# Attention and gated layer in one kernel: ACT's casts behind the copies of sums, output DMAs behind their copies, a tile's third bank last

## Chip, cores and metric

The kernel runs on one NeuronCore of one Trainium2 chip. The metric is the device time of one execution in microseconds (us), the median of several runs. Each execution that was profiled also leaves a trace of every instruction on the engines: TensorE (PE; its weight loads are listed as PEld), VectorE (DVE), ScalarE (ACT), GpSimd (POOL) and SyncE (SP), which issues DMAs. "ACTq" and "SPq" are an engine's sequencer, which issues DMAs and waits.

## The reference

```python
# q, k, v: (8, 8, 576, 64) float32;  w_in: (512, 2048);  w_out: (2048, 512)
scores = np.matmul(q, k.transpose(0, 1, 3, 2)) / 8
scores = np.where(block(row) >= block(column), scores, -1e9)      # blocks of 64
attn = softmax(scores)                                            # over the last axis
x = np.matmul(attn, v)  ->  tokens (4608, 512): head outputs side by side
h = x @ w_in
g = h * (1 / (1 + np.exp(-1.702 * h)))
out = g @ w_out                                                   # (4608, 512) float32
```

## The kernel before, in words

**Two streams of work.** The attention handles 32 pairs of heads (`NPAIR`), four pairs (`HP`) for each of the eight batch entries. The second layer handles 12 tiles of 384 tokens (`TILES`), each with 16 groups (`fc`) of 128 of the 2048 hidden columns. TensorE's order of both is fixed by the program: every matmul is pinned behind the one written before it (`mm`). The main loop writes the items of a pair (from strings such as `ORDER`), and after each item lets the generator `moe()` run until its quota of work is used up, so both streams alternate on TensorE.

**Attention, a step.** Pairs 0 to 7 are "early", pairs 8 to 31 "late". In a late step `n`, TensorE computes scores of chunks 3, 0, 2, 1 of pair `n`; then `N` and `T` scale and turn the weights of what was scored; then `V` is `av(n - 1)`: 60 matmuls of turned weights with values into two sum banks `o0` and `o`, and behind them the scores of chunk 4 of the next pair `m`, part of them into free columns of the same two banks. Then ACT copies the sums from `o0` and `o` to `xr` (L550, L551), SP loads the next values (L309, L312), and `settle(m, [[4]], ...)` handles the scores of chunk 4: for each head DVE's score reduction with mask and maximum (L432), ACT's exp with row sum (L439). In `settle` before the change, `prep(n + 1)` is called after these, ahead of scaling (L448 to L460) and turning (L467, L472 on DVE, then 16 DMAs on SP, L479, into `turned`).

**Preparing queries and keys.** For pairs 9 to 31, `prep` is `prep_late`: for queries (x = 0) and keys (x = 1) DVE transposes the raw data (L322, into `qt` and over `raw`), ACT casts to the rounded half `high` (L323), and POOL subtracts to get `low` in two pieces (L88, `low<-qt,high` and `low<-raw,high`). Score matmuls use both halves in three products. Then `prep` has SP load the raw data of a later pair (L301, eight DMAs).

**The second layer, a tile.** `split(t)` makes the halves `xh` (ACT, L602) and `xl` (DVE, L88) of the tile's tokens from `xr`. For each group `fc`, twelve matmuls go into `hp` (four column blocks with `xh` twice and `xl` once; in group 0 those with `xl` come last); ACT makes a tanh of it (L666), DVE the gated `g` (L667), ACT the rounded half `gh` (L675), POOL the rest `gl` (L88). One group later, `second` adds nine matmuls into the sums `acc0`, `acc1`, `acc2`, three 128-token banks, three products each: `gh` with `woh`, `gh` with `wol`, `gl` with `woh`. In all groups but the last, the six with `gh` come first and the three with `gl` behind them. After the last group each bank is copied to an output tile `osb` by ACT (L632), and ACT issues the DMA to HBM (L634). There are two `osb` buffers, and a third for the last tile only. The next tile uses the same three banks.

**What sets the order on the other engines.** The order of instructions of ACT, DVE, POOL and SP is made when the kernel is built, by a planner: it goes through the program with estimated durations and, whenever an engine is free, takes the ready instruction of highest priority. Earlier written means higher priority, and `high_priority(offset=300)` (around `split`, the tanh, `g`, `gh` and `gl`) treats an instruction as if it were written 300 places earlier. An instruction whose data are ready early in the planner's view can so be placed ahead of others that were written before it. `tc.keep_in_program_order(x)` pins `x` behind the last instruction written before it on the same engine, in issue order only. On the chip each engine then executes that order, and waits on semaphores for data, free buffers and DMA landings.

Of the kernel before, what the change touches and what calls it, by code (L numbers as in the profile page):

```python
# [41 lines left out]
def attention_moe_kernel(  # L42
# [9 lines left out]
    nc = tc.nc  # L52
    B, H, S, D = q.shape
    DM, DF = w_in.shape
    P = 128
# [8 lines left out]
    NPAIR = B * H // 2  # L64
# [8 lines left out]
    def f(ap):  # L73
        return ap.bitcast(F32)
# [59 lines left out]
    def room(tag, shape, dt, name):  # L134
        return d2.tile(shape, dt, tag=tag, name=name, bufs=1)
# [62 lines left out]
    for g in range(NG):  # L198
# [3 lines left out]
        for fc in range(FG):  # L202
            r = (g * FG + fc) * P
# [31 lines left out]
    bits, whole = {}, {}  # L235
# [78 lines left out]
    high, low = {}, {}  # L314

    def prep_late(n):

        high[n] = [room(t, [P, S], F32R, "high") for t in ("wm", "high")]
        low[n] = room("qk", [P, 2, S], F32R, "low")
        for x in range(2):  # L320
            whole = raw[n][:, 0].rearrange("p c d -> p (c d)") if x else room("e1", [P, S], F32, "qt")
            nc.vector.transpose(out=whole, in_=raw[n][:, x].rearrange("p c d -> p (c d)"))  # L322
            nc.scalar.copy(out=high[n][x], in_=whole)  # L323
            for c in (slice(0, S // 2), slice(S // 2, S)):
                subtract(nc.gpsimd, low[n][:, x, c], whole[:, c], f(high[n][x])[:, c])

# [15 lines left out]
    def prep(n):  # L342

        if not parts_of(n):
            qk[n] = room("e0" if n % 2 else "qk", [P, 2, S], F32, "qk")
            for x in range(2):
                nc.vector.transpose(out=qk[n][:, x], in_=raw[n][:, x].rearrange("p c d -> p (c d)"))
        else:
            prep_late(n)
        raw.pop(n)  # L350
        m = follower(n)
        if m is not None:
            load(m)
# [30 lines left out]
    def settle(n, banks, todo):  # L384
        for chunks, part in zip(banks, todo):
            e = {}
            for i, hd, lo, hi, s in part:
                if i not in e:
                    e[i] = es[i] if early(n) else weights_of(n, i)
                weigh(n, i, hd, lo, hi, s, e[i])  # L390
            if early(n):
                for i in chunks[::-1]:
                    if n == 2 * HP - 1 and i == NCH - 1:
                        with tc.high_priority(offset=300):
                            normalise(n, i, e[i])
                    else:
                        normalise(n, i, e[i])
            else:
                weighed.extend((n, i, e[i]) for i in chunks[::-1])
            if 4 in chunks and not early(n):  # L400
                if n + 1 < NPAIR:
                    prep(n + 1)
                normalise_all()
                turn_all()

# [105 lines left out]
    def av(n):  # L511

        b, h = divmod(n, HP)
        before_av(n)
        if turns["late"]:
            o0, o = bank(), bank()
            cut = BLK + 2 * P
        else:
            o, o0 = bank(), bank()
            cut = BLK  # L520

        def place(q0):
            return (o0, q0) if q0 < cut else (o, q0 - cut)

        todo = []
        for i in range(1, NCH):
            bk, c = place((i - 1) * P + BLK)
            todo += [(bk, c, P, j, pw[:, :, SLOT[i] + j]) for j in range(i)]
            todo.append((bk, c + BLK, BLK, i, pw[:, 2:4, 9 + i]))
        todo.append((*place(0), BLK, 0, pw[:, 0:2, 10]))  # L530

        ends = [[x for x, y in enumerate(todo) if y[0] is bk] for bk in (o0, o)]
        for x, (bk, c, nn, j, w) in enumerate(todo):
            for hd in range(2):
                mm(
                    out=bk[hd * D : hd * D + D, c : c + nn].rearrange("d (a c) -> d a c", c=32),
                    lhsT=values(n)[:, hd, j], rhs=w[:, :, hd],
                    start=any(x == y[0] for y in ends), stop=any(x == y[-1] for y in ends),
                )
        m = n + 1  # L540
        rest = []
        if turns["late"] and m < NPAIR:
            own = [lent_bank(), bank()]
            a, z = qrange(4)
            beside = [o0[:, cut : cut + S - K4], o[:, S - cut : S - cut + S - K4]]
            for ss, lo, hi in (([x[:, 0:K4] for x in own], 0, K4), (beside, K4, S)):
                score_into(m, a, ss, lo, hi)
                rest += [(4, hd, lo, hi, ss[hd][0 : z - a]) for hd in range(2)]
        c0 = (b % 2) * S
        nc.scalar.copy(out=xr[:, h, c0 : c0 + cut], in_=o0[:, 0:cut])  # L550
        nc.scalar.copy(out=xr[:, h, c0 + cut : c0 + S], in_=o[:, 0 : S - cut])  # L551
        nxt = follower(n)
        if nxt is not None:
            load_v(nxt)
        if rest:
            settle(m, [[4]], [sorted(rest, key=lambda x: x[2])])

    def follower(n):
# [54 lines left out]
    def moe():  # L613
        prev = None

        def second(state):
            g_hi, g_lo, fc, acc, t = state
            todo = [(c, ga, wb) for c in range(TILES[t][1] // P) for ga, wb in ((g_hi, "woh"), (g_hi, "wol"), (g_lo, "woh"))]
            if fc < NFC - 1:

                todo.sort(key=lambda x: x[1] is g_lo)
            begun = set()
            for x, (c, ga, wb) in enumerate(todo):
                last = ga is g_lo
                mm(
                    out=acc[c], lhsT=ga[:, c * P : (c + 1) * P], rhs=weights(wb, fc // FG)[:, fc % FG],
                    start=fc == 0 and c not in begun, stop=fc == NFC - 1 and last,
                )
                begun.add(c)
                if fc == NFC - 1 and last:  # L630
                    osb = out_room([P, DM], F32, "osb", t == NT - 1)
                    nc.scalar.copy(out=osb, in_=acc[c])  # L632
                    r = TILES[t][0] + c * P
                    nc.scalar.dma_start(out=out[r : r + P, :], in_=osb)  # L634
                if x % 3 == 2:
                    yield 650

        for t in range(NT):
            tt = TILES[t][1]
            if t == 0:  # L640
                yield ("tile", 0)
                split(0)
            xh, xl = xs["xh"], xs["xl"]
            acc = [ps.tile([P, DM], F32, tag=f"acc{c}", name=f"acc{c}") for c in range(tt // P)]
            for fc in range(NFC):
                if t == 0:
                    convert(fc // FG * GROUP + NDC + fc % FG + 1)
                hp = next_hp()
                fs = slice(fc % FG * P, (fc % FG + 1) * P)
                terms = [(wa, xb, dc) for dc in range(NDC) for wa, xb in (("wih", xh), ("wil", xh), ("wih", xl))]  # L650
                if fc == 0:

                    terms.sort(key=lambda x: x[1] is xl)
                for cnt, (wa, xb, dc) in enumerate(terms):
                    mm(
                        out=hp[:, 0:tt], lhsT=weights(wa, fc // FG)[:, dc, fs], rhs=xb[:, dc, 0:tt],
                        start=cnt == 0, stop=cnt == 3 * NDC - 1,
                    )
                    if cnt % 3 == 2:
                        yield unit1(tt)  # L660
                g = d2.tile([P, TT], F32, tag="g", name="g", bufs=1)[:, 0:tt]
                gh = d2.tile([P, TT], F32R, tag="gh", name="gh")[:, 0:tt]
                gl = d2.tile([P, TT], F32R, tag="gl", name="gl")[:, 0:tt]

                with tc.high_priority(offset=300):
                    nc.scalar.activation(out=g, in_=hp[:, 0:tt], func=AF.Tanh, scale=1.702)  # L666
                    nc.vector.scalar_tensor_tensor(  # L667
                        out=g, in0=g, scalar=1.0, in1=hp[:, 0:tt], op0=ALU.add, op1=ALU.mult
                    )

                if fc == NFC - 1 and t + 1 < NT:
                    yield ("tile", t + 1)
                    split(t + 1)
                with tc.high_priority(offset=300):
                    nc.scalar.copy(out=gh, in_=g)  # L675
                    subtract(nc.gpsimd, gl, g, f(gh))
                yield ("gate", fc)
                if prev is not None:
                    yield from second(prev)
                prev = (gh, gl, fc, acc, t)  # L680
        yield from second(prev)


# [85 lines left out]
```

## Time and profile before

| | |
|---|---|
| median of 3 runs | 1099.38 us (1098.8 to 1101.41) |
| the profiled execution's own time | 1097.82 us |
| its span, first to last instruction | 1096.0 us |
| granted TensorE clock, mean | 0.991 |
| busy: PE, PEld, DVE, ACT, POOL | 1058.2, 928.2, 597.5, 522.0, 477.9 us |
| HBM read, written | 45.09 MB, 9.44 MB |

Busy time is a share of the whole span, over stages with different limits. A row of an instruction group or of the timeline names line, engine, operation, `out<-in` tiles and shapes; the bracket at its end is the idle time of the engine just before it and what ended that. A helper's line stands for all its callers: L114 is every matmul, L88 every subtraction. In a row of stretches stand the length, then busy time and number of instructions of PE, PEld, DVE, ACT and POOL, then the granted clock, the DMA share and GB/s. A row of waits names who waited for whom, then the total in us, how often, and the longest.

### The profile page before, as it was taken

The page shows a single profiled execution, that of the slowest core. Times are in us where ns is not written, and L with a number is a line of the kernel's source. Part 1 is how long each engine was busy: PE and PEld are TensorE (multiplying, and loading weights), DVE is VectorE, ACT ScalarE, POOL GpSimd, SP SyncE. Part 2 cuts the span into 40 slices and gives each one's busy share as a digit, 9 for nine tenths or more (in the row PEclk, how much of TensorE's full clock was granted, in tenths as well). Part 3 has the DMA queues.
Part 4 walks back from the last instruction along what each step waited for, and adds up shares of the span by engine and source line. Part 5 has one row for each costly group of instructions (what it writes and reads, how often), then busy time and mean ns, then how long its engine had stood idle before and what let it go on. Part 6 is the DMA issues. An engine that isn't in the chain of part 4 may idle for free. (4 is left out here: it accounts for less than half of the span.)

```text
span 1096.0 us, 20723 instructions
## 1 busy us (share of the span) xinstructions
PE 1058.2 (97%) x7236; PEld 928.2 (85%) x7236; DVE 597.5 (55%) x1856; ACT 522.0 (48%) x1367; POOL 477.9 (44%) x601
## 2 busy tenths in 40 slices
PE   5869999999999999999999999999999999999998
PEld 3647777888889888899898888998898888999997
DVE  6786786755655656655655665655556655211111
ACT  5866776533544544534444543443544443322322
POOL 4665665534444444344344443443444343222222
PEclk9979999999999999999999999999999999999999
DMA  8735523433333443332434343333444322200000
GB/s 174 210 91 156 151 60 81 98 69 80 92 79 77 111 92 79 83 82 67 105 81 87 85 107 62 78 89 76 106 97 88 66 79 48 55 30 1 30 1 30
DMA packets 219369, 91.30 MB, mean 83 GB/s; under 512 B 197760, under 2 KB 197760, under 8 KB 219264
## 3 DMA queue, kind: packets, MB, share of 16 engines
q1 hardware_dynamic: 209344, 79.94, 32.3%
q10 hardware_dynamic: 9920, 10.03, 2.6%
q8 instruction: 57, 0.93, 0.4%
q14 instruction: 48, 0.39, 0.1%
HBM read 45.09 MB, written 9.44 MB: 50 GB/s over the span
## 5 line engine op out<-in xcount | busy, mean ns | idle before, releaser
L88 POOL TENSOR_TENSOR gl<-g,gh 128x384 fp32r<-128x384 f32 x192 | 195.0, 1016 | 454.5 <-ACT gh L675 442.4
L667 DVE SCALAR_TENSOR_TENSOR g<-g,hp 128x384 f32<-128x384 f32 x192 | 104.9, 546 | 359.7 <-ACT g L666 359.6
L114 PE MATMUL hp<-xh,wih 128*128 128x384 f32 x768 | 260.9, 340 | 4.5 <-DVE g L667 2.2
L114 PE MATMUL hp<-xh,wil 128*128 128x384 f32 x768 | 258.3, 336 | 0.0
L114 PE MATMUL hp<-xl,wih 128*128 128x384 f32 x768 | 254.3, 338 | 0.1
L114 PE MATMUL acc<-woh,gh 128*128 128x512 f32 x576 | 232.8, 404 | 2.7 <-ACT osb L632 2.2
L114 PE MATMUL acc<-wol,gh 128*128 128x512 f32 x576 | 227.5, 395 | 0.0
L666 ACT ACTIVATE g<-hp 128x384 f32<-128x384 f32 x192 | 93.7, 488 | 247.5 <-PE hp L114 215.4
L675 ACT CAST gh<-g 128x384 fp32r<-128x384 f32 x192 | 98.5, 513 | 167.9 <-DVE g L667 167.3
L114 PE MATMUL acc<-woh,gl 128*128 128x512 f32 x576 | 168.7, 394 | 0.3 <-POOL gl L88 0.3
L114 PEld LDWEIGHTS hp<-xh,wih 128*128 128x128 f32 x768 | 144.5, 188 | 17.9 <-issue 3.3
L114 PEld LDWEIGHTS hp<-xh,wil 128*128 128x128 f32 x768 | 144.3, 188 | 7.7
L114 PEld LDWEIGHTS hp<-xl,wih 128*128 128x128 f32 x768 | 143.7, 188 | 1.1 <-DVE xl L88 1.1
L439 ACT ACTIVATE e<-e,mx 64x64 f32<-64x64 f32 (+4 forms) x240 | 132.4, 554 | 18.4 <-DVE mx L432 18.4
L114 PEld LDWEIGHTS acc<-woh,gh 128*128 128x128 f32 x576 | 108.0, 188 | 27.1 <-ACT osb L632 4.0
L114 PEld LDWEIGHTS acc<-woh,gl 128*128 128x128 f32 x576 | 107.6, 188 | 25.9 <-POOL gl L88 2.1
L458 POOL TENSOR_TENSOR e<-e,sm 64x64 f32<-64x64 f32 (+1 forms) x192 | 112.9, 613 | 34.0 <-DVE sm L453 23.1
L114 PEld LDWEIGHTS acc<-wol,gh 128*128 128x128 f32 x576 | 108.4, 188 | 16.9 <-issue 0.4
L448 DVE TENSOR_SCALAR sm<-sm 128x2 f32<-128x2 f32 (+1 forms) x160 | 64.6, 404 | 63.6 <-ACT e L439 57.3
L432 DVE CUSTOM_DVE_ANT_0 e<-bank,mask 64x64 f32<-64x64 f32 (+4 forms) x240 | 93.2, 438 | 4.8 <-PE bank L114 4.6
L114 PEld LDWEIGHTS bank<-turned,vp 128*64 128x64 f32 x1800 | 85.4, 137 | 9.6 <-issue 6.6
L114 PE MATMUL bank<-turned,vp 128*64 128x128 f32 (+1 forms) x1800 | 89.6, 257 | 1.6 <-ACT turned L493 1.6
(62 smaller groups left out, 1205.1 us busy)
## 6 DMA issues: line engine op xcount, KB each, us to landing
turned<-turned SPq DMA_DIRECT2D x192, 80.0 KB, 2.1
turned<-turned SPq DMA_DIRECT2D x96, 112.0 KB, 2.2
raw<-in_q_dram SPq DMA_DIRECT2D x128, 72.0 KB, 2.3
out_dram<-osb ACTq DMA_DIRECT2D x36, 256.0 KB, 2.1
raw<-in_k_dram SPq DMA_DIRECT2D x120, 72.0 KB, 2.4
turned<-turned SPq DMA_DIRECT2D x96, 88.0 KB, 2.1
words<-in_moe_w_in_dram SPq DMA_DIRECT2D x16, 512.0 KB, 5.9
vp<-in_v_dram SPq DMA_DIRECT2D x60, 128.0 KB, 2.5
```

The source lines that it names most:

```text
L88: eng.tensor_tensor(out=out, in0=in0, in1=in1, op=ALU.subtract)
L114: return tc.keep_in_program_order(nc.tensor.matmul(**kw))
L432: nc.vector.tensor_tensor_reduce(out=e[0:m, hd, lo:hi], in0=s, in1=mk, op0=ALU.add, op1=ALU.min, scale=-0.125, scalar=3e38 if lo == 0 else ...
L439: nc.scalar.activation(out=e[0:m, hd], in_=e[0:m, hd], func=AF.Exp, scale=-1.0, bias=mx[0:m, i, hd : hd + 1], accum_out=sm[0:m, i, hd : hd ...
L448: x = nc.vector.tensor_scalar(out=c, in0=c, scalar1=1e-9, scalar2=2.0, op0=ALU.add, op1=ALU.mult)
L458: nc.gpsimd.tensor_tensor(out=x, in0=x, in1=sc.to_broadcast([m, width(i)]), op=ALU.mult)
L666: nc.scalar.activation(out=g, in_=hp[:, 0:tt], func=AF.Tanh, scale=1.702)
L667: nc.vector.scalar_tensor_tensor(out=g, in0=g, scalar=1.0, in1=hp[:, 0:tt], op0=ALU.add, op1=ALU.mult)
L675: nc.scalar.copy(out=gh, in_=g)
```

## The change

The casts L323 are pinned behind what is written before them on ACT. `prep(m + 1)` moves from `settle` to `av`, to the place just behind the copies of the sums and the loading of values, ahead of `settle`; so the last ACT instruction written before the first cast is the copy L551. In group 0 of a tile, `second` takes the three products of bank 2 behind all six of banks 0 and 1 (their `gh` products first, then their two `gl` products, then bank 2's). The output DMAs L634 are pinned behind what is written before them on ACT, their own copy.

```diff
@@ prep_late
-            nc.scalar.copy(out=high[n][x], in_=whole)
+            tc.keep_in_program_order(nc.scalar.copy(out=high[n][x], in_=whole))
@@ settle
             if 4 in chunks and not early(n):
-                if n + 1 < NPAIR:
-                    prep(n + 1)
                 normalise_all()
                 turn_all()
@@ av
         if rest:
+            if m + 1 < NPAIR:
+                prep(m + 1)
             settle(m, [[4]], [sorted(rest, key=lambda x: x[2])])
@@ second
             if fc < NFC - 1:
-                todo.sort(key=lambda x: x[1] is g_lo)
+                todo.sort(key=lambda x: (fc == 0 and x[0] == 2, x[1] is g_lo))
@@ second, after the last group
-                    nc.scalar.dma_start(out=out[r : r + P, :], in_=osb)
+                    tc.keep_in_program_order(nc.scalar.dma_start(out=out[r : r + P, :], in_=osb))
```

## The prediction

> **What bounds the kernel now.** I read the page's first part, then busy time by stretches, then TensorE's waits.
>
> ```profile
> span 1096.0 us, 20723 instructions
> PE 1058.2 (97%) x7236; PEld 928.2 (85%) x7236; DVE 597.5 (55%) x1856; ACT 522.0 (48%) x1367; POOL 477.9 (44%) x601
> ```
> ```profile
> 0.00:190.00 190.00, 161.19 (x1173) 124.75 (x1174) 140.99 (x434) 132.71 (x369) 113.04 (x141) 0.96 0.53 133
> 190.00:1050.00 860.00, 855.02 (x5859) 766.42 (x5859) 450.92 (x1413) 377.62 (x977) 354.73 (x451) 1.00 0.33 76
> ```
>
> TensorE (PE, the first busy number of each row) is the bound; ScalarE (ACT) works under half the time. Of the 37.8 us in which PE is idle, 28.8 lie before 190 us, and 4.0 after 1050, where only the last tile runs and no wait is touched. Before 190 the change alters only the order of nine matmuls of tile 0: casts in halves begin with pair 9, output copies with the end of tile 0, and both come after 190. From 190 to 1050, where nearly all edits act, PE is idle for 860.00 - 855.02 = 5.0 us. So the gain is capped near 5 us, 0.45%. What TensorE waits for in that stretch:
>
> ```profile
> PE acc L114 <- ACT osb L632: 2.2, 3, 0.8
> PE hp L114 <- ACT xh L602: 1.6, 1, 1.6
> ```
>
> The first is the output sums' third bank, not yet copied out when the next tile wants it; the second is one wait at tile 1's start. Together 3.8 of the 5.0 us, and each has an edit aimed at it.
>
> **The third bank (edit at L621).** The three waits are at tiles 3, 6 and 9 and alike (2.2 us over three, the longest 0.8). Tile 3, on ACT, POOL and PE (start, duration):
>
> ```profile
> 374.32 0.56 ACT L632 COPY osb<-acc 128x512 f32<-128x512 f32 x1
> 375.24 0.51 ACT L675 CAST gh<-g 128x384 fp32r<-128x384 f32 x1 [0.36 <-DVE g L667]
> 375.30 0.34 ACTq L634 DMA_DIRECT2D out_dram<-osb  x1
> 375.68 0.59 ACT L632 COPY osb<-acc 128x512 f32<-128x512 f32 x1
> 376.30 0.34 ACTq L634 DMA_DIRECT2D out_dram<-osb  x1
> 377.37 0.58 ACT L632 COPY osb<-acc 128x512 f32<-128x512 f32 x1 [1.10 <-DMA out_dram<-osb]
> ```
> ```profile
> 376.31 1.01 POOL L88 TENSOR_TENSOR gl<-g,gh 128x384 fp32r<-128x384 f32 x1
> ```
> ```profile
> 376.87 0.39 PE L114 MATMUL acc<-wol,gh 128*128 128x512 f32 x1
> 378.00 0.51 PE L114 MATMUL acc<-woh,gh 128*128 128x512 f32 x1 [0.75 <-ACT osb L632]
> 378.34 0.40 PE L114 MATMUL acc<-wol,gh 128*128 128x512 f32 x1
> 378.58 0.86 PE L114 MATMUL acc<-woh,gl 128*128 128x512 f32 x3
> 379.29 0.33 PE L114 MATMUL hp<-xh,wih 128*128 128x384 f32 x1
> ```
>
> Matmuls into the sums start every 0.24 us (378.34 to 378.58); the first after a wait takes 0.34 (378.00 to 378.34). The third bank is wanted at 376.87 + 0.24 = 377.11, fifth in order; its copy ends at 377.95, and PE starts 378.00. With the edit, fifth and sixth are the matmuls with gl for banks 0 and 1, and the third bank is wanted two steps later. But gl ends at 376.31 + 1.01 = 377.32, not by 377.11: a new wait of about 0.26 takes part of the old one's place. Then 377.37, 377.71 and, at 377.95, the third bank, whose copy ends just then: start 378.00, after it 0.34, 0.24, 0.24 to the group's end at 378.82 instead of 379.29. Gain 0.47 a tile. Had the copy come earlier (next part), the end would be 378.67 and the gain 0.62. In the other tiles PE shows no wait for the copy, so nothing is gained, and gl is made long before the new fifth matmul, so nothing is lost. Sum: 3 x 0.47 = 1.4 us.
>
> **Output DMAs behind their copies (L634).** The edit pins a DMA behind the last ACT instruction written before it, which is its own copy; by data it follows it already. In the rows above the first DMA stands behind copy and gh cast: the copy ended 374.88, gh waited for VectorE until 375.24, the DMA left at 375.30. If the pin changes nothing, 0. If the DMAs move right behind their copies, that one leaves at 374.92, lands 0.38 earlier, and the third copy, which waits for that landing, starts 0.38 earlier: 0.15 more per tile. The price is that ACT, which issues in order, stands until the copy has ended and the DMA is out (0.34); behind the third copy waits the next tanh, 0.5 us later, whose gh is needed only after the next hp group, the twelve matmuls that start at 379.29 in the rows. I take 0, since the pin adds no order that the data do not, and keep 3 x 0.15 = 0.45 us of gain for the range.
>
> **Casts pinned, prep earlier (L323, L554).** What moves: per late pair two DVE transposes, two ACT casts, four POOL subtractions, eight raw loads on SP. Where it matters once, at tile 1's start (ACT, PE, DVE):
>
> ```profile
> 197.89 0.51 ACT L675 CAST gh<-g 128x384 fp32r<-128x384 f32 x1 [3.65 <-DVE g L667]
> 199.71 0.67 ACT L323 CAST high<-qt 128x576 fp32r<-128x576 f32 x1 [1.30 <-DVE qt L322]
> 200.52 0.67 ACT L323 CAST high<-raw 128x576 fp32r<-128x576 f32 x1
> 201.10 0.42 ACT L550 COPY xr<-bank 128x320 f32<-128x320 f32 x1
> 201.41 0.38 ACT L551 COPY xr<-bank 128x256 f32<-128x256 f32 x1
> 201.68 0.52 ACT L602 CAST xh<-xr 128x384 fp32r<-128x384 f32 x1
> ```
> ```profile
> 196.10 1.24 PE L114 MATMUL bank<-qk 64*128 64x384 f32 x8
> ```
> ```profile
> 200.33 0.34 PE L114 MATMUL hp<-xh,wil 128*128 128x384 f32 x1
> 202.25 0.44 PE L114 MATMUL hp<-xh,wih 128*128 128x384 f32 x1 [1.58 <-ACT xh L602]
> ```
> ```profile
> 202.23 0.94 DVE L88 TENSOR_TENSOR xl<-xr,xh 128x384 fp32r<-128x384 f32 x1
> ```
>
> The sums were ready at 197.34, yet their copies stand behind two casts that wait for transposes; the xh cast that TensorE needs stands behind the copies. With the casts after the copies, gh ends 198.40, copies 199.1, xh 199.6: ready before PE wants it at 200.50, and 202.25 - 200.50 = 1.75 us go. What is late next is xl, made on DVE: wanted at 201.4 (200.50, two matmuls and three of xl at 0.175), now begun at 202.23 behind the chunk's score reductions (L432). If it keeps its place, it ends about 202.5 (two of those reductions wait less for the copies), so 1.1 us stay and 0.65 are gained; if it goes ahead of them, all 1.75. I take 1.0, nearer the lower end: the first two reductions are ready with the scores, before the copies are.
>
> In the other 22 late steps the copies also wait for a cast. One step:
>
> ```profile
> 514.77 0.27 PE L114 MATMUL bank<-low,high 64*128 64x192 f32 x2
> ```
> ```profile
> 515.81 0.68 ACT L323 CAST high<-raw 128x576 fp32r<-128x576 f32 x1 [2.99 <-DMA vp<-in_v_dram]
> ```
> ```profile
> 517.55 0.79 ACT L439 ACTIVATE e<-e,mx 128x576 f32<-128x576 f32 x1
> ```
>
> ACT is idle 2.99 us ahead of the cast, yet PE runs on with earlier groups. The scores end at 515.04, so copies would run 515.1 to 515.8, casts to 517.0, and the exp starts 0.3 to 0.5 us earlier than 517.55. No TensorE wait hangs on it: 0. The raw key goes from first to second cast, its subtractions and the raw loads behind them on SP up to 1.5 us later, with the 16 turning DMAs queued behind; they are read a step later, so 0 again, but see the last rival.
>
> **The sum.** 1.4 + 1.0 = 2.4 us: span 1096.0 to 1093.6, profiled time 1097.82 to 1095.4. The median of the runs, 1099.38, lies 1.56 above the profiled one: 1097.0, or -0.22%. The ends: 0.65 + 1.4 = 2.05 us and 1.75 + 1.4 + 0.45 = 3.6 us.
>
> **Rivals.** A difference within 0.3% (3.3 us) is about what a measurement of this kernel cannot tell from no change.
>
> (1) Full gain. DMAs leave right behind their copies and xl runs promptly: 3.6 us, and with the small waits of the stretch (5.0 - 3.8 = 1.2, if they end on ACT's chains) up to 4.8. Time 1094.6 to 1095.8. For it: ACT has room, and these waits are most of what is left. Against it: nothing forces xl ahead of the reductions.
>
> (2) Hidden anyway. The third copy slips by the 0.3 to 0.5 us that ACT stands at DMAs, and new short waits on gl and xl stay: gain 0 to 1 us, 1098.4 to 1099.4. For it: gl is already late by 0.2 at the three tiles.
>
> (3) Slower, by one mechanism: the turning DMAs on SP (L479) held by an output's DMA.
>
> ```profile
> SPq L479 <- DMA out_dram<-osb: 31.1, 12, 7.0
> ```
> ```profile
> 364.64 18.85 SPq L479 DMA_DIRECT2D turned<-turned  x16
> ```
> ```profile
> 616.40 18.66 SPq L479 DMA_DIRECT2D turned<-turned  x16
> ```
> ```profile
> turned<-turned SPq DMA_DIRECT2D x192, 80.0 KB, 2.1
> ```
> ```profile
> 385.67 2.99 PE L114 MATMUL bank<-turned,vp 128*64 128x128 f32 x60
> ```
> ```profile
> DMA to landing us min/median/max: 2.0/2.1/4.4
> ```
>
> At tiles 3 and 6 the sixteen take over 18 us because they stand up to 7.0 us until an output DMA has landed. At tile 3 the last is issued some 0.6 us before 383.49 and lands 2.1 later, at 385.0: 0.65 us before TensorE reads it. If the pins rearrange the queues so that SP waits for the third output's DMA (after the third copy, at 377.95 or later) and not the first's (375.30), and that DMA takes the longest landing of the outputs (the last row), 4.4 us instead of 2.0, the turned weights come 2.65 + 2.4 = 5.05 us later and TensorE stands 4.4 us at each of two tiles: 8.8 - 2.4 = +6.4, 1105.8. It decides beyond 0.65 us of delay, and outweighs the gains where the delay passes 1.85 us. Against it: with the first output DMA's place unchanged, SP waits as now.
>
> ```profile
> 60.00:65.00 5.00, 2.08 (x12) 1.64 (x10) 3.51 (x7) 2.45 (x6) 3.17 (x3) 0.50 0.88 138
> ```
> ```profile
> PE bank L117 <- ACT xr L550: 2.9, 1, 2.9
> ```
>
> TensorE's clock would make such stalls dearer: in the stretch from 60 to 65 us, with a wait of 2.9 us in it, the granted clock is 0.50, and five us at half speed cost up to 2.5 more, so 5 over both tiles and 1110.8. The Trainium skill, "TensorE: Matmul & The Clock Gate", section "HAM oscillation — how this bites in real kernels", sets the limit at idle gaps of about 3.4 us: by it a stall of 4.4 slows the clock too, but one under 3.4 costs only itself. The trace is the harsher of the two, as its 2.9 us were enough after an earlier idle spell. Either way the waits of today's late part, under 2 us, stand at clock 1.00, and the forecast's sum gets nothing from the clock.
>
> **How the numbers follow.** Forecast (2.05 to 3.3 us gained) 0.51, full gain 0.27, hidden 0.11, slower 0.11. Predicted 1097.0. Faster by over 0.3%: the full gain and the forecast's edge, 0.33; slower 0.11; the rest 0.56. The range leaves out the slow case and the full gain's last part: 1094.3 to 1100.4, where the top takes in the hidden case and the scatter of the runs shown.
>
> **What would show it.** Right: the wait of acc for osb at tiles 3, 6, 9 gone, a wait for gl of 0.2 to 0.3 there; on ACT, L550 and L551 ahead of both casts in every late step; hp's wait for xh at 200 us gone or replaced by one for xl under 1.1; PE idle between 190 and 1050 near 2.6 us. Wrong: PE waits at av's first matmul, or idle time elsewhere that the planner's new order made.

## The result, and the profile after

The changed kernel takes 1105.76 us (median of 6 runs, 1104.23 to 1107.27) against 1098.7 us for the kernel before beside it (6 runs): ratio 1.0063, 95% interval 1.005 to 1.0075. The forecast was 1097.0 us in a range of 1094.3 to 1100.4, so it was wrong, in sign too. The rival on the slower side, with a chance of 0.11, had 1105.8.

The profiled execution of the kernel after took 1107.27 us, the slowest of the six; so the two profiled executions lie 9.45 us apart and the medians 7.06. Its first lines, then busy time by stretches:

```profile
span 1105.5 us, 20704 instructions
PE 1061.2 (96%) x7236; PEld 933.4 (84%) x7236; DVE 594.8 (54%) x1856; ACT 526.3 (48%) x1367; POOL 477.5 (43%) x601
```
```profile
0.00:190.00 190.00, 161.42 (x1174) 124.83 (x1174) 140.99 (x436) 133.10 (x371) 113.46 (x142) 0.96 0.53 133
190.00:1050.00 860.00, 848.38 (x5810) 762.94 (x5810) 447.12 (x1409) 379.48 (x971) 351.81 (x448) 0.99 0.33 76
```

The first stretch is as before. From 190 to 1050 us TensorE's idle time goes from 5.0 to 11.6 us, and the mean clock from 1.00 to 0.99. What TensorE waits for there, from its list of waits, and two rows of SP's list:

```profile
PE bank L114 <- DMA turned<-turned: 9.2, 4, 3.6
...
PE hp L114 <- DVE xl L88: 1.7, 1, 1.7
```
```profile
SPq L301 <- POOL low L88: 57.2, 22, 2.9
SPq L477 <- DMA out_dram<-osb: 48.0, 12, 9.9
```

The three waits for `osb` and the one for `xh` are gone. In their place stand one for `xl` and, new, four at the first matmul of `av`, for the DMAs that turn the weights: 2.30 us at tile 2, 1.12 at tile 3, 2.21 at tile 5 and 3.57 at tile 8. SP (L477 is L479 of before) now stands 48.0 us ahead of these DMAs until an output's DMA has landed; before it was 31.1.

Tile 2 shows the whole chain. The sixteen turning DMAs of that step, before and after, then the last two of them after:

```profile
271.01 10.06 SPq L479 DMA_DIRECT2D turned<-turned  x16
```
```profile
270.54 18.90 SPq L477 DMA_DIRECT2D turned<-turned  x16
```
```profile
288.30 1.14 SPq L477 DMA_DIRECT2D turned<-turned  x2
```

They start 0.5 us earlier than before, and still the last leaves 8 us later: fourteen go out one behind the other, and two stand until 288.30. ACT and PE of the kernel after at that moment:

```profile
285.64 0.59 ACT L632 COPY osb<-acc 128x512 f32<-128x512 f32 x1
286.12 0.52 ACT L675 CAST gh<-g 128x384 fp32r<-128x384 f32 x1
286.25 0.34 ACTq L634 DMA_DIRECT2D out_dram<-osb  x1
...
288.36 0.59 ACT L632 COPY osb<-acc 128x512 f32<-128x512 f32 x1 [1.08 <-DMA out_dram<-osb]
```
```profile
291.39 4.63 PE L114 MATMUL bank<-turned,vp 128*64 128x128 f32 x60 [2.30 <-DMA turned<-turned]
```

The first output DMA leaves at 286.25. Its landing frees the buffer for ACT's third copy at 288.36, and at the same moment SP's two turning DMAs go. The second of them is out at 289.44 and lands some 2 us later, and TensorE starts at 291.39. No data tie a turning DMA to an output. What ties them is the built program, in which this can be read: every DMA of SP and of ACT reports its completion on one of eight semaphores, handed out in turn in the planner's order, and a DMA waits until the one before it on its semaphore has landed. In the kernel before, the next user of the first output's semaphore at tile 2 is a load of values; in the kernel after it is the fifteenth of the sixteen turning DMAs.

The 60 matmuls then take 4.63 us; in the row of before they took 2.99. The granted clock (third number from the end) in the stretches after this wait and after the one at tile 5:

```profile
292.00:294.00 2.00, 2.00 (x32) 2.00 (x29) 2.00 (x6) 0.00 (x0) 0.00 (x0) 0.61 0.03 8
294.00:296.00 2.00, 2.00 (x26) 1.92 (x22) 0.78 (x1) 0.00 (x0) 0.00 (x0) 0.54 0.00 0
...
548.00:550.00 2.00, 2.00 (x31) 2.00 (x28) 1.97 (x7) 0.00 (x0) 0.00 (x0) 0.61 0.03 8
550.00:552.00 2.00, 2.00 (x23) 1.88 (x22) 0.67 (x1) 0.00 (x0) 0.00 (x0) 0.54 0.00 0
```

Each of the three waits over 2 us is followed by some 3.4 us at half clock, 1.64 us of extra work at tile 2. Of the span's 9.5 us more (1105.5 - 1096.0), 6.6 us are idle time. Three such spells would add about 3 x 1.64 = 4.9 us, but TensorE's busy time grew by 3.0 only (1058.2 to 1061.2); the ends of matmuls are modelled, and I do not split the rest further.

### The profile page after: what moved, and what is told of

It reads as the page before. It is cut to its first block, busy times and chain, and to the rows that moved or that the text cites. A ratio compares the mean times of both kernels' runs of the same rounds, so it can differ in the third digit from the quotient of the medians.

```text
span 1105.5 us, 20704 instructions
## 1 busy us (share of the span) xinstructions
PE 1061.2 (96%) x7236; PEld 933.4 (84%) x7236; DVE 594.8 (54%) x1856; ACT 526.3 (48%) x1367; POOL 477.5 (43%) x601
## 4 chain that ended last, share of the span: by engine, by line
PE 86%; DVE 4%; DMA 3%; ACT 3%; issue 2%; SPq 1%; POOL 1%; POOLq 0%; ACTq 0%; DVEq 0%
PE acc L114 34%; PE hp L114 34%; PE bank L114 16%; DMA out_dram<-osb 1%; PE bank L117 1%; ACT turned L437 1%; DMA turned<-turned 1%; DVE wm L256 1%; DMA raw<-in_k_dram 1%; DVE turned L430 1%; DVE qk L347 0%; DVE xl L88 0%; ACT e L437 0%; DMA words<-in_moe_w_out_dram 0%; DVE wm L251 0%
## 5 line engine op out<-in xcount | busy, mean ns | idle before, releaser
L114 PEld LDWEIGHTS bank<-turned,vp 128*64 128x64 f32 x1800 | 90.3, 142 | 19.3 <-issue 15.7
L114 PE MATMUL bank<-turned,vp 128*64 128x128 f32 (+1 forms) x1800 | 94.4, 265 | 11.1 <-DMA turned<-turned 9.2
L446 DVE TENSOR_SCALAR sm<-sm 128x2 f32<-128x2 f32 (+1 forms) x160 | 61.1, 382 | 59.4 <-ACT e L437 53.2
## 6 DMA issues: line engine op xcount, KB each, us to landing
out_dram<-osb ACTq DMA_DIRECT2D x36, 256.0 KB, 2.1
```

Of the source, the lines that this page charges most:

```text
L114: return tc.keep_in_program_order(nc.tensor.matmul(**kw))
L446: x = nc.vector.tensor_scalar(out=c, in0=c, scalar1=1e-9, scalar2=2.0, op0=ALU.add, op1=ALU.mult)
```

## The experiments

The theory: the new order of DMAs lets an output's completion semaphore fall on one of the last turning DMAs, and that, with the clock behind it, is the loss. The main rival: the pinned casts make the subtractions and so the raw loads on SP later (57.2 us of waits for `low`, before 36.1), and these push the turning DMAs. Letters in the quoted expectations are explained in each. "Before" in the first four is 1099.05 us (28 runs), in the next four 1099.04 us (21 runs).

### The third bank last, alone

```diff
-                todo.sort(key=lambda x: x[1] is g_lo)
+                todo.sort(key=lambda x: (fc == 0 and x[0] == 2, x[1] is g_lo))
```

> The kernel before with the third bank last alone (L621); every other engine's order stays as before. Theory A (the shared completion semaphores of DMAs, moved by the pinned casts, are the loss): no wait of TensorE at av's first matmul, the osb waits of 0.75 at tiles 3, 6, 9 become waits for gl of about 0.26, 1.4 us faster than before. Rival B (the new order of banks, by letting copies and outputs run at other times, makes the waits): waits for turned weights at tiles 2, 5, 8 of over 2 us, and at least 4 us slower than before.

Measured: 1098.65 us (12 runs), ratio 0.9991 (0.9981 to 1.0001). Of TensorE's waits:

```profile
PE bank L114 <- DMA turned<-turned: 0.6, 1, 0.6
```

The waits for `osb` are gone. But at tile 6 TensorE, now earlier, meets the turning DMAs: 0.6 us. A gain of 0.4 us remains by the medians (1.0 by the ratio), within what can be told from none. So the edit does no harm, and the loss is not here.

### The casts pinned and the preparation moved, alone

```diff
-            nc.scalar.copy(out=high[n][x], in_=whole)
+            tc.keep_in_program_order(nc.scalar.copy(out=high[n][x], in_=whole))
@@ prep(n + 1) from settle to av, as in the change
```

> The kernel before with the casts pinned and prep moved alone (L323, L554). Theory A: the last two turning DMAs of the steps at tiles 2, 5 and 8 wait for an output DMA, TensorE waits 2 to 3.6 us for turned weights there and 1.1 at tile 3, and runs at half clock for some 3 us after each; 7 to 8 us slower than before, so up to 1.4 us above the changed kernel. Rival B (bank order): within 1 us of before.

Measured: 1104.78 us (8 runs), ratio 1.0043 (1.0028 to 1.0059). Of TensorE's waits:

```profile
PE bank L114 <- DMA turned<-turned: 6.6, 3, 2.3
```

Waits of 2.31, 2.23 and 2.05 us at tiles 2, 5 and 8: the loss comes with these two edits alone. The waits for `osb` are gone here too, with the third bank in its old place. So in the changed kernel the bank's edit had nothing left to remove. The built program has the changed kernel's order on every engine but TensorE, so the pin of the output DMAs, left out here, moves nothing.

### The changed kernel, output DMAs issued by POOL

```diff
-                    tc.keep_in_program_order(nc.scalar.dma_start(out=out[r : r + P, :], in_=osb))
+                    nc.gpsimd.dma_start(out=out[r : r + P, :], in_=osb)
```

In the built program POOL's DMAs have semaphores of their own, so no turning DMA shares one with an output. The orders of SP, DVE and TensorE are those of the changed kernel.

> The changed kernel, but the output DMAs are issued by POOL, whose DMAs complete on other semaphores than SP's and ACT's. Theory A: no turning DMA waits for an output any more, the waits for turned weights at tiles 2, 3, 5, 8 go (over 9 us of waits and half clock), and the time is 2 to 3 us under before, less whatever POOL's issuing costs gl. Rival C (raw loads on SP come 1.5 us later, and the turning DMAs are late for that alone): the waits stay, and the time is that of the changed kernel, about 1105.

Measured: 1102.74 us (12 runs), ratio 1.0029 (1.0018 to 1.0041). SP's waits for the raw loads, the turning DMAs at tile 2, and TensorE's wait:

```profile
SPq L301 <- POOL low L88: 56.5, 22, 2.9
```
```profile
271.93 10.07 SPq L477 DMA_DIRECT2D turned<-turned  x16
```
```profile
PE acc L114 <- ACT osb L632: 4.6, 3, 2.2
```

The raw loads are as late as in the changed kernel (56.5 against 57.2 us), yet the sixteen go out in 10.07 us as before, and every wait at `av` is gone. That takes the raw-load rival away. The time is no win, since POOL issues the outputs later (at tile 3 the first one 1.4 us after its copy, in the changed kernel 0.4) and ACT's copies wait for `osb` buffers instead: 4.6 us of TensorE's waits at tiles 3, 6 and 9.

### The changed kernel, raw loads behind the turning DMAs

The edit, abridged:

```diff
@@ prep
-        m = follower(n)
-        if m is not None:
-            load(m)
+        if not (n > 2 * HP):
+            load_next(n)          # load_next(n): load(follower(n))
@@ settle
                 turn_all()
+                if n + 1 < NPAIR:
+                    load_next(n + 1)
```

> The changed kernel, but the eight raw loads of the next pair are written behind the turning of the weights, so that SP issues the sixteen turning DMAs first. Theory A: by the order built, no turning DMA of the steps at tiles 2, 3, 5, 6, 8, 9 takes its completion semaphore behind an output; waits for turned weights gone, 2 to 3 us under before. Rival D (raw loads that stand behind an output come too late for the transposes): waits on scores or exps appear in the steps of tiles 3, 6, 9, and the time is above before.

Measured: 1097.18 us (9 runs), ratio 0.9973 (0.9963 to 0.9983), span 1094.5 us. By the medians it beats the kernel before by 1.9 us (by the ratio 3.0) and the changed kernel by 8.6. Of TensorE's waits in the late part one over 0.5 us is left, that for `xl` of 1.7 us. SP's wait with the raw loads, and the turning DMAs at tile 2:

```profile
SPq L301 <- DMA out_dram<-osb: 24.5, 7, 7.6
```
```profile
269.99 10.06 SPq L483 DMA_DIRECT2D turned<-turned  x16
```

In the built program the outputs' semaphores now pass to raw loads and loads of values at tiles 2, 3, 5, 6, 8 and 9. SP still stands up to 7.6 us behind an output, but what stands is not wanted soon, and the edits' own gain appears. The edit moves loads of SP alone, but the planner, given another program, also orders DVE, ACT and POOL otherwise. So it is the run with POOL's outputs that singles out the semaphores, and this one shows that a reorder can avoid them.

### The casts pinned, nothing else

```diff
-            nc.scalar.copy(out=high[n][x], in_=whole)
+            tc.keep_in_program_order(nc.scalar.copy(out=high[n][x], in_=whole))
```

> Only the casts of queries and keys are pinned behind the copies of sums (L323); prep stays where it was, the third bank and the outputs' DMAs are as before. Theory A (a turning DMA on SP stands until an output's DMA with the same completion semaphore has landed): in this kernel's order the two first output DMAs of a tile share their semaphores with the turning DMAs 13 and 15 of the step, not 14 alone, so TensorE's wait at the first matmul of av at tiles 2, 5 and 8 is longer than the 2.2 to 2.3 us of the casts with prep moved: about 3.3 us, each with some four us at half clock behind it: 1106 to 1109 us. Theory B (the raw loads, which come later on SP, hold the turning DMAs): nothing but the pins counts, so the waits and the time are those of the run with casts pinned and prep moved, 1103 to 1106 us. If neither holds, prep's move alone was the harm: about 1099 us.

Measured: 1124.13 us (4 runs), ratio 1.0231 (1.0216 to 1.0246). At tile 2, the turning DMAs behind the landing, and TensorE:

```profile
296.58 1.77 SPq L479 DMA_DIRECT2D turned<-turned  x3
```
```profile
300.66 4.64 PE L114 MATMUL bank<-turned,vp 128*64 128x128 f32 x60 [3.26 <-DMA turned<-turned]
```
```profile
PE bank L114 <- POOL low L88: 2.0, 2, 1.0
```

Three of sixteen stand behind the output, and the waits are 3.26, 3.19 and 3.10 us: the mechanism as expected. The time is 15 us past the expectation. Casts pinned without the earlier preparation are late also for the next scores (2.0 us at tile 1, with half clock behind them) and for ACT's output copies (waits for `osb` of 3.2 us at four places). The move of the preparation was needed to make the pins bearable.

### The changed kernel, keys' cast first

The edit, abridged:

```diff
         for x in range(2):
             whole = ...; transpose            # both first
+            wholes.append(whole)
+        for x in (1, 0):
+            whole = wholes[x]
             cast L323; subtractions
```

> The changed kernel with the keys' cast and subtractions ahead of the queries' in each pair. The next user of the first output's semaphore is now turning DMA 15, the last one, in place of 14. Theory A: one DMA issue (0.55 us) less stands behind the landing, so the waits at av at tiles 2, 5 and 8 shrink from 2.2 to 2.3 us to 1.6 to 1.8 us (tile 8, where the landing was late, to about 3.0); where the wait is under about 2 us the granted clock stays at 1.00, which saves 1.6 us a tile more. Time 1101 to 1104 us. Theory B: the raw key is free about 0.7 us earlier, so the raw loads go out earlier and all waits at av go: 1096 to 1099 us. If the order of casts doesn't matter: 1105 to 1106 us.

Measured: 1099.2 us (11 runs), ratio 1.0005 (0.9995 to 1.0015). At tile 2, the turning DMA behind the landing, TensorE, and the clock after it:

```profile
289.09 0.51 SPq L481 DMA_DIRECT2D turned<-turned  x1
```
```profile
291.48 2.98 PE L114 MATMUL bank<-turned,vp 128*64 128x128 f32 x60 [1.59 <-DMA turned<-turned]
```
```profile
292.00:294.00 2.00, 2.00 (x45) 2.00 (x43) 2.00 (x6) 0.00 (x0) 0.69 (x1) 1.00 0.04 8
```

One turning DMA stands behind the landing in place of two. The waits are 1.59, 1.41 and 1.27 us, the clock stays at 1.00, and the 60 matmuls take 2.98 us again. The time lies in the rival's range and below the 1101 to 1104 that I gave the theory, but the rival wanted no waits at `av`, and they are there. I had the total too dear: the wait of 1.12 us at tile 3 went as well, that at tile 8 was 1.27 us and not about 3.0, and the wait for `xl` at tile 1 fell from 1.73 to 1.1.

| kernel | turning DMAs behind the landing | waits at tiles 2, 5, 8, us | time less before, us |
|---|---|---|---|
| before | 0 | none | 0 |
| keys' cast first | 1 | 1.59, 1.41, 1.27 | +0.2 |
| casts and preparation | 2 | 2.31, 2.23, 2.05 | +5.7 |
| the change | 2 | 2.30, 2.21, 3.57 | +7.1 |
| casts pinned only | 3 | 3.26, 3.19, 3.10 | +25.1, of which part by late casts |

Each turning DMA more is 0.7 to 1.0 us more of wait at tile 2, somewhat more than the 0.57 us that SP takes to issue one (1.14 for two). What makes up the rest was not taken apart.

### Raw loads behind the turning DMAs: with the third bank alone, with the casts alone

```diff
@@ first: before + third bank last + the loads' move of above
@@ second: the changed kernel with the loads' move, third bank and output DMAs as before
```

> The kernel before with the third bank last and with the raw loads of the next pair issued behind the turning DMAs; no cast is pinned. Theory A: the waits for the third bank go (about 0.13 us each stays on gl), and the two short waits at av that the third bank alone had at tiles 3 and 6 (0.08 and 0.62 us) go too, since turning DMAs are held at the last one at most; the wait for xh at tile 1 stays at 1.6 us. 1097 to 1098.5 us. Rival (the pins are needed for the gain of the raw loads' move): 1098.5 to 1099.5 us.

> Casts pinned and prep moved, raw loads of the next pair behind the turning DMAs, but the third bank in its old place. Theory A: no output DMA shares its semaphore with the tail of the turning DMAs, so no wait at av; the pinned casts alone already bring the copies of the output sums in time, so the third bank's old place costs nothing: 1096.5 to 1098 us, the same as with the third bank last. Rival (the third bank's edit is still worth its 0.5 us a tile once the casts are pinned): waits of TensorE for osb at tiles 3, 6 and 9 come back, 1098 to 1099 us.

Measured: the first 1104.38 us (5 runs), ratio 1.005 (1.0036 to 1.0064); the second 1098.24 us (11 runs), ratio 0.9993 (0.9984 to 1.0002). TensorE's waits of the first, then of the second:

```profile
PE acc L114 <- ACT gh L681: 2.7, 2, 1.6
```
```profile
PE acc L114 <- ACT osb L638: 1.3, 3, 0.7
```

The first misses its expectation by 6 us, on the far side of the rival: with the raw loads later and the casts in their old place, the second layer waits for `gh` and the next scores for `low` (1.5 us). TensorE's idle time from 190 to 1050 us is 7.6 us where it was 5.0, so these waits are about half of the 5.3 us lost, and the other half is open. The loads' move pays only together with the change's casts. The second supports its rival: the waits for `osb` come back (1.3 us), and the third bank's edit is worth about 1.1 us once the rest is in order (1098.24 less 1097.18, against kernels before that lie 0.01 us apart; by the two ratios, 0.9993 and 0.9973, it is 2.2). In the built programs the two versions differ in TensorE's order alone.

### Keys' cast first and raw loads behind the turning DMAs

> The changed kernel with both: the raw loads of the next pair behind the turning DMAs, and the keys' cast and subtractions ahead of the queries'. Theory A: no wait at av at tiles 2, 5 and 8, because the outputs' semaphores pass to raw and value loads there (at tile 9 the last turning DMA shares one, which costs 0.3 us at most); at tile 1's start the wait for xl is 1.1 us, as with the keys first alone, in place of 1.73. So 0.65 us under the loads-last version's 1097.2: 1096.0 to 1097.0 us. Rival (the later cast of the queries delays the next step's scores): 1097.5 to 1099 us, with new waits of TensorE for high or low of the queries.

Measured: 1136.48 us (5 runs) against 1099.71 us, ratio 1.0334 (1.0315 to 1.0352). Of TensorE's waits:

```profile
PE bank L114 <- POOL low L88: 22.8, 13, 2.9
```

The wait for `xl` is 1.1 us as expected, and no wait at `av` is left. But the scores wait in 13 steps for `low` of the queries, which came last of a preparation that was late already: that is the rival, but some 39 us above the version with the loads last, where I had put 0.3 to 1.8. The loads' move uses up the slack of the preparation, and the order of casts then matters.

## Why the prediction was wrong, step by step

**The bound and the cap.** TensorE's 5.0 us of idle time did cap the gain: the best version takes 1.9 us off by the medians, 3.0 by the ratio. A cap on gains says nothing of losses.

**The third bank.** This term was right in mechanism and in size at each tile. With the edit alone, tile 3 reads:

```profile
379.25 0.39 PE L114 MATMUL acc<-wol,gh 128*128 128x512 f32 x1
379.77 0.73 PE L114 MATMUL acc<-woh,gl 128*128 128x512 f32 x2
...
381.19 0.34 PE L114 MATMUL hp<-xh,wih 128*128 128x384 f32 x1
```

From the fourth matmul to the group's end it is 1.94 us, before 2.42 (376.87 to 379.29): 0.48 gained where 0.47 was forecast, and likewise 0.46 and 0.47 at tiles 6 and 9. The new wait on `gl` makes the fifth matmul 0.28 us late (379.77 for 379.25 + 0.24), where I had 0.26. What the term left out came behind it: a TensorE that is earlier at tile 6 runs into the turning DMAs, for 0.62 us. The prediction had seen that such a wait is 0.65 us away at tile 3, and used this for the rival only. In time the gain was 0.4 us by the medians, with an interval from 2.1 us gained to 0.1 lost. In the whole change it gave nothing: with the casts and the preparation alone the waits for `osb` were gone too. Why they then come back in part with the loads moved (1.3 us) is open.

**The output DMAs' pin.** This was worth 0, as forecast. In the rows of tile 2 the DMA still leaves behind the `gh` cast (286.12, then 286.25). The pin was not run by itself, but the program built with it alone has the same order on every engine as the kernel before.

**Tile 1's start.** This term was mis-sized: 1.0 us was forecast, and nothing came of it. ACT did what was said, DVE did not:

```profile
198.23 0.38 ACT L549 COPY xr<-bank 128x256 f32<-128x256 f32 x1
198.50 0.53 ACT L602 CAST xh<-xr 128x384 fp32r<-128x384 f32 x1
```
```profile
199.31 0.78 DVE L322 STREAM_TRANSPOSE raw<-raw 128x576 f32<-128x576 f32 x1
200.01 0.52 DVE L430 CUSTOM_DVE_ANT_0 e<-bank,mask 128x384 f32<-128x384 f32 x1
...
201.62 1.18 DVE L88 TENSOR_TENSOR xl<-xr,xh 128x384 fp32r<-128x384 f32 x1
```
```profile
202.85 0.45 PE L114 MATMUL hp<-xl,wih 128*128 128x384 f32 x1 [1.73 <-DVE xl L88]
```

The copies stand ahead of `xh` and the casts behind it, and `xh` is ready at 199.03. But `xl` ends at 202.80, wanted at 201.12. I had it end 0.67 us sooner (203.17 to 202.5), as two of the score reductions ahead of it would wait less for the copies. They had waited only 0.2 us for them; for the rest transposes and reductions follow each other on DVE without a gap, in both kernels in the same order. The first reduction starts 0.4 us earlier than before, as this whole start does, and `xl` starts 0.2 earlier than that, but it takes 1.18 us in place of 0.94. So the wait for `xh` of 1.58 became one for `xl` of 1.73. Whether `xl` placed ahead of the reductions would bring the 1.75 us is open; it was not tried. The version with the keys' cast first brought it to 1.1.

**The other 22 steps.** This is the step that failed. The words "they are read a step later, so 0 again" price the raw loads and the turning DMAs by their data alone. The order of SP's DMAs among ACT's also decides which semaphore each shares, and that was not in the sum. In place of 0 the runs showed waits for turned weights of 2.30, 1.12, 2.21 and 3.57 us, 9.2 in all, and half clock behind three of them. I had its sign in view: SP's 31.1 us of waits for outputs were quoted for the rival, and the answer to them was that the first output DMA's place is unchanged. It was, nearly. What moved was which turning DMA stands behind it, and at which tile.

**The slower rival.** It was right in mechanism (a turning DMA held by an output's DMA) and nearly in time (1105.8 for 1105.76), but this is partly luck. It named tiles 3 and 6 with 4.4 us each; it was tiles 2, 5 and 8 with 2.2 to 3.6 us, half clock behind each, and 1.12 us at tile 3. Its condition was that SP should come to wait for the third output and not the first. In the kernel before that was so already, at tile 3 (ACT's third output, then SP's last turning DMAs):

```profile
377.98 0.35 ACTq L634 DMA_DIRECT2D out_dram<-osb  x1
```
```profile
382.36 1.14 SPq L479 DMA_DIRECT2D turned<-turned  x2
```

That output took 4.4 us to land, to 382.38, and in the built program the fifteenth turning DMA has its semaphore. So the delay that the rival feared was part of the 18.85 us that it quoted, and the 0.65 us of margin were left behind it. In the changed kernel the first output is enough, where it falls on one of the last turning DMAs. The rival's chance of 0.11 was too low, for 12 such waits stood in the profile before, and their places hang on the order that the change rewrites.

**The clock.** The harsher reading held, though the row that it rested on was misread. In the kernel before half clock began at 59.99 us, and the wait of 2.9 us only at 60.54:

```profile
56.57:59.99 3.42, 1.00 (x11) 0.94 (x12) 2.95 (x6) 1.15 (x2) 2.56 (x4) 1.00 0.01 1
59.99:63.40 3.41, 0.55 (x4) 0.15 (x1) 2.06 (x4) 1.74 (x5) 2.96 (x3) 0.50 0.83 135
```
```profile
63.46 2.37 PE L117 MATMUL bank<-ident,turned 128*128 128x128 f32 x10 [2.92 <-ACT xr L550]
```

So it was the idle time ahead of it, 2.42 of 3.42 us, that half clock followed. The Trainium skill, "TensorE: Matmul & The Clock Gate", section "HAM oscillation — how this bites in real kernels", warns of idle gaps over about 3.4 us; by that limit two of the changed kernel's three waits over 2 us would have cost nothing more. The trace differs: waits of 2.30 and 2.21 us were followed by clocks of 0.61 and 0.54.

## What to carry to other kernels

Before moving an instruction in one engine's order, list the DMAs that move with it, and for each queue which earlier DMA each one waits for, data or not: a bookkeeping semaphore shared by two queues is as real a wait as a buffer. Where a row says that a queue waits for a transfer it has no data from, ask which of its DMAs stands there and how soon that one is read; slack there is what a reorder spends first. Put what is read last at the end of the queue, and then measure the pair of edits together, since here the casts alone, the loads' move with the old casts, and the loads' move with another order of casts were each slower than before.

## What the runs showed of the hardware

The granted clock does not follow the length of a wait alone. In the late part of these kernels all waits of 2.9 us and more were followed by half clock. Of those from 1.9 to 2.4 us, seven were and four were not: in the casts' run 2.31 and 2.05 us were, and this one was not:

```profile
546.71 2.98 PE L114 MATMUL bank<-turned,vp 128*64 128x128 f32 x60 [2.23 <-DMA turned<-turned]
```
```profile
544.93:548.34 3.41, 1.63 (x35) 1.66 (x37) 2.33 (x7) 0.65 (x2) 1.00 (x1) 1.00 0.41 122
548.34:551.75 3.41, 3.41 (x48) 3.06 (x45) 3.03 (x8) 0.98 (x3) 0.00 (x0) 1.00 0.08 20
```

Of 27 from 1.0 to 1.8 us one by itself was, 1.57 us in the last run, and in the run with the casts pinned only three of 0.4 to 1.0 us close together. In the changed kernel the two stretches at 292 and 548 us have the same two clocks, 0.61 and 0.54, so the slow spells lie 256.0 us apart to within some hundredths, and the third, at 804.43 us, 256.0 behind the second (548.43). The waits ahead of them end 255.85 and 256.33 us apart, so it is not they that set this distance. The Trainium skill, "TensorE: Matmul & The Clock Gate", section "What's actually happening", describes a free-running window of 3.413 us; 256.0 us are 75.0 of these. By that rule the phase of a wait decides along with its length, and the trace agrees with the phase, but not with a full idle window as the condition: 2.3 us were enough.

The two can be put together. The slow spells start and end on a grid of 3.41 us. The window of it that ends at 292.43 us in the changed kernel, and the one behind it:

```profile
289.02:292.43 3.41, 1.11 (x24) 1.07 (x25) 1.72 (x5) 1.00 (x2) 1.00 (x1) 1.00 0.44 133
292.43:295.84 3.41, 3.41 (x43) 3.41 (x38) 2.35 (x6) 0.00 (x0) 0.00 (x0) 0.50 0.00 0
```

Here all 2.30 us of the wait lie in one window. In the casts' run only 1.78 of the 2.23 us do (3.41 - 1.63, in the row from 544.93), and the clock stays at 1.00. Take this grid from a slow spell of each of the eleven profiled executions, from 190 to 1090 us. Then each of the 11 windows at full clock in which TensorE was idle for 1.9 us or more is followed by one at half clock. Of the 34 with 1.0 to 1.8 us three were (1.47, 1.57 and 1.64 us, all with scores that waited for `low`); what sets these three apart is open.
